# The first three blocks of a fused attention and MLP kernel, issued from one list of single operations

## The chip, the core and the metric

The kernel runs on one core of one Trainium2 chip. The core has four engines that matter here, each working through its own instructions in a fixed order: TensorE (PE in the profile) multiplies, VectorE (DVE) and ScalarE (ACT) do elementwise work, and SyncE (SP) issues the DMAs. They wait for one another through semaphores. The metric is the device time of one execution in microseconds. Before the change three runs took 893.93, 894.45 and 894.88 us, median 894.45.

## The reference

The input has 4 sequences of 576 positions, 8 heads of 64; together 2304 tokens of width 512. A windowed attention (each position sees itself and the 63 before it) is followed by two MLPs with a hidden width of 2048:

```python
mask = (rel >= 0) & (rel < 64)
attn = softmax(where(mask, q @ k.T / 8, -1e9));  x = attn @ v        # 2304 x 512
x = (maximum(x @ moe_w_in, 0) ** 2) @ moe_w_out
h = x @ moe2_w_in
out = where(h > 0, h, exp(minimum(h, 0)) - 1) @ moe2_w_out
```

The four weight matrices arrive as 64-bit floats, and the kernel decodes each one on the chip. Every matmul operand of the MLPs is split into a high and a low part, so one product is three matmuls (high by high, high by low, low by high).

## The kernel before

**Blocks.** The tokens go through in five blocks of 512, 256, 512, 512 and 512. The attention of a block is done in four head pairs ("groups" in the order list, numbered 0 to 19 over all five blocks). A group has its scores on PE (64 by 128 matmuls, `s_half`), a maximum of each 128 by 128 tile on DVE (`s_max`), the exponential on ACT (`s_exp`), the division on DVE, transposes on PE (`s_T`) with copies out of PSUM, the product with v on PE (`s_V`), and a split into high and low (`s_X`).

**First MLP.** The first three blocks go through the first MLP in the plain way, 16 chunks j of the hidden width each: `h_chunk` (4 of them, 12 matmuls) makes the hidden values in a PSUM bank, `h_relu`, `h_square` and the high half of `h_split` follow on ACT and the low half on DVE, and two chunks later `o_chunk` (4, 12 matmuls) adds the product with w_out onto four accumulators. From the sixth chunk of the first block on, every hidden chunk uses the same PSUM bank, so the hidden matmuls of the next chunk start only when the relu of this one has read the bank. The attention of blocks 4 and 5 is also done beside the third block, and those two blocks then go through the first MLP together, as seven products on sums of quarters instead of eight (`stepw`, operands `X`, results copied by ACT to tiles named `tl`). All later work, the rest of the first MLP and the second MLP, follows that.

**Weights of the second MLP.** Beside the blocks the kernel prepares weights in "portions" (`portions`, 105 of them): for each of 8 column pairs it forms seven quarter sums of the first MLP's w_in, and for each of 16 tasks it fetches a second-MLP weight in four pieces of 256 KB from DRAM into a landing place (a "lane"), decodes each (`high16` on ACT, `join` on DVE), forms sums on DVE, splits them (high on ACT, low on DVE) in a staging place and writes them back to DRAM. A piece's lane is fetched again as soon as it is decoded.

**What sets the order.** `FIRST` (line 950) is a written list of single operations for the first block's attention and its first six chunks. From there the loop at line 1078 emits code chunk by chunk: the four `h_chunk`, relu, square and split, a whole attention group (`group`, `turned`) at the chunks named in `GRP`, and whole portions (`slot`) as `SLOTS` says: 4 portions in the first block, 21 in the second and 30 in the third, of which 21 are in its last seven chunks:

```python
    SLOTS = {(0, NJ - 2): 2, (0, NJ - 1): 2}
    SLOTS |= {(1, j): 2 if j in (5, 6, 9, 10, 13) else 1 for j in range(NJ)}
    SLOTS |= {(TW, j): 1 if j < 9 else 3 for j in range(NJ)}
```

While `pinned` holds, every instruction is chained behind the one emitted before it on its engine (`Noted`), so each engine runs exactly in the order of emission; DMAs are chained on SP in the same way. A portion is emitted whole: its sums, its high parts and its low parts stand next to each other on DVE and ACT. Behind the third block the pins are off, and the framework's scheduler places the remaining portions among the `stepw` products. The lanes are half of the tile `top`, and two halves of `hw` from the third block on. At a block's end `leave1` copies the four accumulators to tiles (`e_tile`) and stores them to DRAM; two of the tiles share the two buffers named `g` with the relu's output.

Of the kernel before, what the change touches and what calls it, by code (L numbers as in the profile page):

```python
# [10 lines left out]
F32 = mybir.dt.float32  # L11
# [8 lines left out]
P = 128  # L20
# [3 lines left out]
ORDER2 = [0, 2, 3, 4, 1]  # L24

@with_exitstack
def window_attention_then_two_mlps(
# [224 lines left out]
    nf = [0]  # L252

    def fetch(x):
        if nf[0] < len(HALVES):
# [3 lines left out]
            lanes.append(x)  # L259

    def more_lanes(*ks):
        if lanes:
            for k in ks:
                fetch(hw[k // 2].bitcast(U16)[:, k % 2].rearrange("p (f w) -> p f w", w=4))

    def sub2(x, a, b, op=ALU.subtract):
        flush()
        vec.tensor_tensor(out=x, in0=a, in1=b, op=op)

    def put(i, p, k, x):  # L270

        m = x.shape[1]
        hi, lo, o = stage(m)
# [5 lines left out]
        def leave():  # L279
# [6 lines left out]
        if i == 1:  # L286
            for n in range(m):
                split(
                    *(z[:, n].rearrange("p (m a j) -> p a m j", m=FT, j=TB) for z in (hi, lo)),
                    x[:, n].rearrange("p (a m j) -> p a m j", m=FT, j=TB), vec,  # L290
                    leave if n == m - 1 else None,
                )
        else:
            split(hi, lo, x, vec, leave)

    def portions():

        y = lane["y"] = wts.tile([P, 2, KD * P], U32, tag="y", name="y")
# [3 lines left out]

        def sums(p, i):
            sub2(q21, q21, q22, ALU.add)
            sub2(q11, q21, q11)
            put(i, p, "s2", left)
            yield
            sub2(right, right, yf[:, 0:1, :HW].broadcast_to([P, 2, HW]))
            put(i, p, "s4", right)
            yield  # L310

        for p in range(NP):
# [3 lines left out]
            for k, j, h in (("a11", p, 0), ("a12", p, 1), ("a22", p + NP, 1)):  # L316
                sp.dma_start(
                    out=wd0[p][:, ORD1.index(k)], in_=wt[j, 0].bitcast(F32)[:, :, h * HW:(h + 1) * HW]
                )
            yield  # L320
            yield from sums(p, 2)
        fetch(top[:, 1].bitcast(U16).rearrange("p (f w) -> p f w", w=4))
        yield
        for n, (i, p) in enumerate(TASKS):
            for r in range(2):
                for h in range(2):
                    c = slice(h * HW, (h + 1) * HW)
                    x = lanes.pop(0)
                    high16(top[:, 0, c], x)

                    def rest(r=r, c=c, x=x):
                        join(y[:, r, c], top[:, 0, c], x)
                        fetch(x)

                    later(rest)
                yield
                flush()
            if i:
                put(i, p, 1, left)
                put(i, p, 3, yf[:, 1:2, HW:])  # L340
                yield
                sub2(q12, q12, q11)
                sub2(q22, q22, q12)
                put(i, p, 5, right)
                yield
                sub2(q11, q22, q11)
                sub2(q21, q21, q22)
                put(i, p, 7, left)
                yield
            else:  # L350
                put(i, p, "a11", yf[:, 0].rearrange("p (k f) -> p k f", k=2))
                put(i, p, "a22", yf[:, 1:2, HW:])
                yield
                yield from sums(p, i)
# [4 lines left out]
    def slot(n=1):  # L359
        for _ in range(n):  # L360
            if pinned:
                flush()
                if next(todo, 0) is None:
                    count[0] += 1
                continue
            with tc.issue_after(last["cd"].ins), tc.issue_after(last["ca"].ins):
                quiet.append(1)
                if next(todo, 0) is None:
                    count[0] += 1
                quiet.pop()  # L370
# [123 lines left out]
    def s_X(u):  # L494
        t, p = u
        n, ps = BLOCKS[t], st.pop(u)["v"]
        if t > TW:
# [3 lines left out]
            if p % 2:  # L501
                later(lambda: copy(XQ[k][:, 1], ps[:, :n], vec))
            else:
                copy(XQ[k][:, 0], ps[:, :n], act)
            return
        s = xs[t, p] = xp.tile([P, 2, NMAX], F32R, tag=f"xs{p}", name="xs")
# [74 lines left out]
    SLOTS = {(0, NJ - 2): 2, (0, NJ - 1): 2}  # L581
    SLOTS |= {(1, j): 2 if j in (5, 6, 9, 10, 13) else 1 for j in range(NJ)}
    SLOTS |= {(TW, j): 1 if j < 9 else 3 for j in range(NJ)}
    GRP = [(0, 4), (0, 6), (0, 8), (0, 10), (0, 12), (0, 13), (0, 15), (1, 3), (1, 7), (1, 11)]
    GRP = {x: n for n, x in enumerate(GRP + [(TW, j) for j in range(8)])}

# [17 lines left out]

    turn = [0, 0]

    def stage(m):

        n = turn[1] = turn[1] + 1
        if lw or hw:  # L610
            if n % 3 == 0 and hw:
                o = hw[1].rearrange("p y f -> p (y f)").rearrange("p (k y f) -> p k y f", k=2, y=2)
            elif lw:
                o = lw[0].tile([P, 2, 2, HW], F32R, tag="wo", name="wo", bufs=2)
            else:
                o = at.tile([P, 2, 2, HW], F32R, tag="wo", name="wo", bufs=1)
            o = o[:, :m]
            return o[:, :, 0], o[:, :, 1], o
        if n % 3 == 0:
            o = at.tile([P, 2, 2, HW], F32R, tag="wo", name="wo", bufs=1)[:, :m]  # L620
            return o[:, :, 0], o[:, :, 1], o
        k = 2 * (n % 3) - 2
        return *(xs[1, (k + r) % KD][:, :m, HW:] for r in range(2)), None
# [55 lines left out]
    def x_make(b, n=NH):  # L679
# [26 lines left out]
        yield  # L706

# [207 lines left out]
    def prod2(b, k, p, lo=0, hi=NH, ms=range(FT)):  # L915
# [28 lines left out]

    vec.memset(top, 0)
# [3 lines left out]
    U = [(0, p) for p in range(HP)]  # L949
    FIRST = """  # L950
        S00 S01 R000 R001 E000 R002 R010 E001 R011 S10 R003 E010 R012 S11 E011 R013 R100 E012 R101 R102
        E013 R110 R111 E110 R112 R103 E111 rc01 E002 D01 E003 top0 R113 T01 rc00 D00 pt01 stt0 E112 T00
        E113 S21 wh00 pt00 wl00 E100 V0 rc11 E101 D11 E102 E103 R210 T11 xhi0 rc10 D10 E210 pt11 R211
        T10 xlo0 E211 S31 pt10 R212 S20 R213 R310 E212 R311 V1 R312 E213 R313 R200 E310 rc21 E200 h00
        R201 D21 xhi1 E201 R202 T21 R203 E202 xlo1 E203 pt21 rc20 h01 D20 E311 S30 E312 T20 R300 E313
        R301 E300 R302 R303 E301 rc31 pt20 D31 E302 V2 E303 top1 rc30 T31 D30 xhi2 stt1 T30 pt31 xlo2
        pt30 wh10 top2 h02 wl10 V3 stt2 h10 xhi3 h11 xlo3 top3 h12 wh21 wl21 h03 wh20 h13 rl0 wl20 h20
        sq0 stt3 gh0 h21 rl1 h22 gl0 top4 h23 wh30 wl30 o00 sq1 wh31 o01 wl31 gh1 o02 rl2 stt4 o03 sq2
        h30 wh41 gh2 h31 gl1 top5 h32 gl2 h33 wl41 o10 wh40 rl3 wl40 o11 sq3 stt5 gh3 o20 o12 wh51 top6
        o13 wl51 o21 wh50 gl3 o22 wl50 o23 stt6 o30 o31 wh60 o32 wh61 wl61 o33 wl60 h40 h50 h51 h52 h53  # L960
        h41 h42 h43 rl4 sq4 gh4 rl5 gl4 sq5 gh5 gl5
    """.split()
    LOADS = {
        "": "0k 0q 1k 1q c 0v w0 2q 2k w1 1v 3q 3k w2 2v w3 3v w4 w5 w6",
        "V1": "4q 4k w7 4v w8 5q 5k w9 5v w10 w11 w12 w13 w14",
        "stt3": "w15 w16",
    }

    def loads(x):
        for x in LOADS.get(x, "").split():  # L970
            if x == "c":
                constants()
            elif x[0] == "w":
                w_load(int(x[1:]))
            else:
                u_load(order[int(x[0])], x[1])

    pinned.append(1)
    loads("")

    def first(x):
        k, a = x.rstrip("0123456789"), [int(i) for i in x.lstrip("abcdefghijklmnopqrstuvwxyzERSTDVX")]
        if k in ("S", "R", "E", "rc", "D", "T", "pt", "V", "xhi", "xlo"):
            u, bank_ = U[a[0]], lambda n=0: ps_o.tile([P, 512], F32, tag=f"o{2 * (a[0] % 2) + n}", name="pa")
        if k == "S":
            s_half(u, a[1], bank_(a[1]))
        elif k in ("R", "E"):
            (s_max if k == "R" else s_exp)(u, *a[1:])
        elif k in ("rc", "D"):
            (s_rc if k == "rc" else s_div)(u, a[1])  # L990
        elif k == "T":
            s_T(u, a[1], bank_(a[1]))
        elif k == "pt":
            s_pt(u, a[1], act)
        elif k == "V":
            s_V(u, bank_())
# [311 lines left out]
```

## Time and profile before

| | us |
|---|---|
| median of three runs | 894.45 |
| the profiled execution | 894.42 |
| its span, first to last instruction | 892.6 |
| PE busy | 832.6 |
| DVE busy | 600.4 |
| ACT busy | 560.9 |

The mean granted clock of PE is 0.971 of full. The profile cuts the span into stretches: the stretch from 0 to 52.25 us is the written list up to the output chunks of the first block's fourth chunk, 149.40 is the first block's end, 228.00 the second's, 356.06 the third's, and at 370.51 the third product of the last two blocks starts. A stretch's busy time on PE can't be read as work done: matmuls overlap in the records, and their recorded length grows when PE waits inside a group. The distance from the start of one group of matmuls to the start of the next, where nothing waits, is the time that the group really takes.

### The profile page before, as it was taken

The page shows a single profiled execution, that of the slowest core. Times are in us where ns is not written, and L with a number is a line of the kernel's source. Part 1 is how long each engine was busy: PE and PEld are TensorE (multiplying, and loading weights), DVE is VectorE, ACT ScalarE, POOL GpSimd, SP SyncE. Part 2 cuts the span into 40 slices and gives each one's busy share as a digit, 9 for nine tenths or more (in the row PEclk, how much of TensorE's full clock was granted, in tenths as well). Part 3 has the DMA queues.
Part 4 walks back from the last instruction along what each step waited for, and adds up shares of the span by engine and source line. Part 5 has one row for each costly group of instructions (what it writes and reads, how often), then busy time and mean ns, then how long its engine had stood idle before and what let it go on. Part 6 is the DMA issues. An engine that isn't in the chain of part 4 may idle for free. (4 is left out here: it accounts for less than half of the span.)

```text
span 892.6 us, 14761 instructions
## 1 busy us (share of the span) xinstructions
PE 832.6 (93%) x5196; PEld 748.0 (84%) x5196; DVE 600.4 (67%) x1403; ACT 560.9 (63%) x1279; POOL 2.1 (0%) x11
## 2 busy tenths in 40 slices
PE   6969997979999966499999999999999999999998
PEld 6757787979888745388888789999999999999998
DVE  6857876666555355657567674769956698666875
ACT  6845665655776354487777555776747766477652
POOL 0000000000000000000000000000000000000000
PEclk9989999998999978699999999999999999999999
DMA  9960127576653564599897969788898778777842
GB/s 346 401 246 28 59 80 249 190 260 216 207 179 96 194 230 156 187 355 357 309 343 253 337 234 311 276 312 265 271 299 272 285 267 277 247 249 289 287 155 54
DMA packets 98682, 214.86 MB, mean 241 GB/s; under 512 B 26544, under 2 KB 53680, under 8 KB 90160
## 3 DMA queue, kind: packets, MB, share of 16 engines
q1 hardware_dynamic: 97776, 213.72, 68.8%
q8 instruction: 41, 0.67, 0.3%
q10 hardware_dynamic: 832, 0.20, 0.1%
q14 instruction: 33, 0.27, 0.1%
HBM read 160.41 MB, written 53.48 MB: 240 GB/s over the span
## 5 line engine op out<-in xcount | busy, mean ns | idle before, releaser
L58 PE MATMUL o<-gs,w 128*128 128x512 f32 (+1 forms) x960 | 223.1, 378 | 1.8 <-ACT ev L58 1.2
L58 PEld LDWEIGHTS o<-gs,w 128*128 128x128 f32 x960 | 168.0, 190 | 35.9 <-ACT ev L58 1.6
L58 PE MATMUL po<-g,wr 128*128 128x384 f32 (+1 forms) x972 | 168.6, 333 | 0.0
L58 PEld LDWEIGHTS po<-g,wr 128*128 128x128 f32 x972 | 167.4, 188 | 0.0
L58 PE MATMUL ph<-xs,w 128*128 128x512 f32 (+1 forms) x576 | 129.7, 376 | 33.2 <-ACT g L58 25.9
L58 PEld LDWEIGHTS ph<-xs,w 128*128 128x128 f32 x576 | 101.1, 199 | 54.4 <-ACT g L58 27.8
L58 ACT ACTIVATE g<-gr 128x384 fp32r<-128x384 f32 x168 | 87.1, 525 | 55.4 <-PE po L58 49.4
L58 DVE TENSOR_TENSOR g<-gr,g 128x384 fp32r<-128x384 f32 x168 | 89.9, 551 | 16.1 <-ACT g L58 15.2
L58 PE MATMUL px<-xo,wr 128*128 128x384 f32 x432 | 83.8, 334 | 0.0
L58 PEld LDWEIGHTS px<-xo,wr 128*128 128x128 f32 x432 | 75.8, 188 | 0.4
L58 DVE TENSOR_TENSOR gs<-g,gs 128x512 fp32r<-128x512 f32 (+1 forms) x64 | 39.8, 623 | 47.5 <-ACT gs L58 47.0
L58 ACT ACTIVATE g<-ph 128x512 f32<-128x512 f32 (+1 forms) x48 | 24.9, 519 | 65.0 <-PE ph L58 54.6
L58 ACT ACTIVATE pb<-pb,nm 128x128 f32<-128x128 f32 x144 | 55.9, 390 | 10.4 <-DVE nm L58 9.4
L58 ACT ACTIVATE sy<-px 128x384 f32<-128x384 f32 x69 | 33.8, 490 | 43.5 <-PE px L58 43.1
L58 PE MATMUL px<-xo,w 128*128 128x512 f32 x192 | 48.2, 399 | 12.9 <-ACT tl L58 12.9
L58 PE MATMUL po<-xo,wr 128*128 128x384 f32 x288 | 56.2, 334 | 0.0
L58 PE MATMUL py<-xo,wr 128*128 128x384 f32 x288 | 55.7, 334 | 0.0
L58 PEld LDWEIGHTS px<-xo,w 128*128 128x128 f32 x192 | 37.1, 194 | 21.3 <-ACT tl L58 13.3
L58 DVE CUSTOM_DVE_ANT_0 pb<-pa,mask 128x128 f32<-128x128 f32 x144 | 32.7, 287 | 29.7 <-PE pa L58 29.6
L58 DVE TENSOR_TENSOR gr<-gr 128x384 f32<-128x384 f32 x96 | 52.1, 552 | 0.5
L58 DVE TENSOR_TENSOR gr<-sy,py 128x384 f32<-128x384 f32 x48 | 26.6, 554 | 36.8 <-PE py L58 23.5
L58 PEld LDWEIGHTS po<-xo,wr 128*128 128x128 f32 x288 | 50.5, 188 | 0.0
(88 smaller groups left out, 1116.9 us busy)
## 6 DMA issues: line engine op xcount, KB each, us to landing
wr<-wd SPq DMA_DIRECT2D x66, 1024.0 KB, 6.3
wd<-wo SPq DMA_DIRECT2D x38, 512.0 KB, 4.3
wr<-wd SPq DMA_DIRECT2D x24, 768.0 KB, 4.6
w<-wd SPq DMA_DIRECT2D x56, 256.0 KB, 5.3
vr<-in_v_dram SPq DMA_DIRECT2D x16, 512.0 KB, 5.2
wraw<-in_moe_w_in_dram SPq DMA_DIRECT2D x16, 511.8 KB, 8.7
wraw<-in_moe_w_out_dram SPq DMA_DIRECT2D x16, 511.8 KB, 9.9
wd<-tl SPq DMA_DIRECT2D x15, 512.0 KB, 4.5
```

The source lines that it names most:

```text
L58: r = fn(*a, **kw)
```

## The change

The written list now covers everything to the end of the third block. `ORDER1` names about 1,500 single operations with their numbers: `Lq.6` loads q of group 6, `S`, `R`, `E`, `rc`, `D`, `T`, `pt`, `V` (or `G`, scores of one group and the v product of another) and `xhi`, `xlo` are an attention group's steps, `top`, `stt`, `wh`, `wl` decode and split a weight unit of the first MLP, `H`, `rl`, `sq`, `gh`, `gl`, `O` are the steps of a chunk (numbered 0 to 47 over three blocks), `ev` and `st` copy and store an accumulator, `P.n` is the n-th single operation of the portions, and `X.n` of the operands of `stepw`. Each is emitted in the list's order and pinned behind its predecessor on its engine. `portions` now gives up control after every operation instead of after every portion.

```diff
+ORDER1 = """
+Lq.0 Lk.0 Lk.1 Lq.1 Lq.3 Lq.2 Lv.3 Lv.1 Lk.3 Lk.2 Lw.0 S.0.1 Lv.0 Lw.1 S.0.0 R.0.1.0 Lw.2 R.0.1.1
...
-    def more_lanes(*ks):
-        if lanes:
-            for k in ks:
-                fetch(hw[k // 2].bitcast(U16)[:, k % 2].rearrange("p (f w) -> p f w", w=4))
+    def lanes_of(kind, x):
+        for k in range(2):
+            fetch((kind, x[:, k * 2 * HW:(k + 1) * 2 * HW].bitcast(U16).rearrange("p (f w) -> p f w", w=4)))
...
+                    high16(top[:, 0, c], x[1])
+                    yield 0
+                    join(y[:, r, c], top[:, 0, c], x[1])
+                    fetch(x)
+                    yield h
...
+    def act_ev(t, m):
+        wait["e", t, m] = e_tile(t, m)
+        copy(wait["e", t, m][:, :BLOCKS[t]], acc[0][m][:, :BLOCKS[t]], vec if m % 2 else act)
...
+    def act_in(k):
+        x = wts.tile([P, 2, 2 * NMAX], F32R, tag=f"in{k}", name="tl")
+        lanes_of(f"in{k}", x[:, 1])
+        lend[f"in{k}"] = x[:, 0].rearrange("p (k y f) -> p k y f", k=2, y=2)
+        places.insert(0, f"in{k}")
+
+    def act_ret():
+        for k in (1, 2):
+            retired.append(f"in{k}")
+            places.remove(f"in{k}")
...
+        "pt": lambda g, n: s_pt(order[g], n, vec if g >= PTD and n else act),
...
+        "H": lambda q, c: h_chunk(*its[q], c, q if q < 4 else int(q == 5)),
...
+    for x in ORDER1.split():
+        name, *a = x.split(".")
+        ACTS[name](*map(int, a))
     assert not wait and not soon
...
-    unit(7)
-    for i, (t, j) in enumerate(its):
...
+    leave1(TW)
     pinned.clear()
     behind2[:] = [last["pe"]]
+    tl.update({k: lw[0].tile([P, NMAX], F32, tag=f"tl{k}", name="tl") for k in (1, 6, 7)})
+    for i in (1, 2):
+        stepw(0, i)
+        slot()
```

Besides the order, the list opens two further weight tiles of the third block (`in1`, `in2`) once their weights are used up, each as two lanes and one staging place (seven lanes in all until `ret`, three after it), and the half rows of the second block's `xs` tiles serve as two staging places from the first portion on. From group 8 on the second copy out of the transposes goes to DVE. 62 portions lie in the list instead of 55. The first two `stepw` products, which stood inside the third block's last chunk, come behind the list. One PSUM bank for the hidden chunks stays as it was.

On ACT near the third block's end, before: `xo<-xr` is an operand of `stepw`, `top<-` decodes a piece, `wo<-y` and `tl<-y` are high parts of a portion, and `g<-ph` is the relu.

```order
L58 ACTIVATE xo<-xr 128x1024 x2
L58 ACTIVATE wo<-y 128x2x256
L58 ACTIVATE wo<-y 128x256
L58 ACTIVATE g<-ph 128x512
L58 ACTIVATE g<-g 128x512
L58 ACTIVATE gs<-g 128x512
L58 ACTIVATE tl<-y 128x2x256
L58 ACTIVATE wo<-y 128x2x256
L58 ACTIVATE top<-top 128x256
L58 ACTIVATE top<-tl 128x256
L58 ACTIVATE g<-ph 128x512
L58 ACTIVATE g<-g 128x512
```

In the list's order, the same engine some chunks earlier in the third block, where the portions' work now lies:

```order
L167 ACTIVATE g<-ph 128x512
L167 ACTIVATE wo<-y 128x256
L167 ACTIVATE g<-g 128x512
L167 ACTIVATE gs<-g 128x512
L167 ACTIVATE xo<-xr 128x1024
L167 ACTIVATE pb,sm<-pb,nm 128x128 x4
L167 ACTIVATE pt<-pa 128x512
L167 ACTIVATE pb,sm<-pb,nm 128x128 x4
L167 ACTIVATE tl<-y 128x2x256
L167 ACTIVATE g<-ph 128x512
L167 ACTIVATE g<-g 128x512
L167 ACTIVATE gs<-g 128x512
```

Two operands of `stepw` and two high parts stood in a row ahead of the first relu here, and four more operations ahead of the next. Now one operand and one high part stand between a split and the next relu, with an attention group's tiles (`pb`, `pt`) between them, and one high part between a relu and its square. Counted over the third block's sixteen relus, the operations of portions and `stepw` between a relu and the one before it were 0 to 2 up to the twelfth chunk and then 8, 4, 7 and 5; now they are 0, 1 and from the third chunk on 2 to 5.

ACT behind the last chunk's split, before, up to the store copies (`ev<-o`) of the accumulators; `tl<-px` is the copy of a `stepw` product:

```order
L58 ACTIVATE top<-tl 128x256 x2
L58 ACTIVATE xo<-xr 128x1024 x3
L58 ACTIVATE tl<-px 128x512
L58 ACTIVATE wo<-y 128x2x256
L58 ACTIVATE wo<-y 128x256
L58 ACTIVATE tl<-y 128x2x256
L58 ACTIVATE tl<-px 128x512
L58 ACTIVATE top<-top 128x256
L58 ACTIVATE top<-tl 128x256
L58 ACTIVATE wo<-y 128x2x256
L58 ACTIVATE ev<-o_2535 128x512
L58 ACTIVATE ev<-o_2537 128x512
```

The same place now:

```order
L167 ACTIVATE wo<-y 128x2x256
L167 ACTIVATE top<-tl 128x256 x3
L167 ACTIVATE tl<-px 128x512
L167 ACTIVATE xo<-xr 128x1024
L167 ACTIVATE top<-top 128x256
L167 ACTIVATE g<-g 128x512
L167 ACTIVATE tl<-px 128x512
L167 ACTIVATE g<-g 128x512
L167 ACTIVATE gs<-g 128x512
L167 ACTIVATE xo<-xr 128x1024
L167 ACTIVATE wo<-y 128x2x256
L167 ACTIVATE tl<-y 128x256
```

The copies `ev<-o` of the accumulators now follow eleven rows below the last one shown. Between the first copy of a product and them stand 21 operations, the copies of three more products among them; before it were seven, with one more product.

## Rows read from the trace of the kernel before

**Rows 1.** Waits of PE over the whole span: who waited for whom, total, times, longest.
```profile
PE ph L58 <- ACT g L58: 25.9, 7, 8.0
PE px L58 <- ACT tl L58: 12.9, 1, 12.9
```
**Rows 2.** Busy time of each engine by stretch; x counts instructions; PEclk is the granted clock.
```profile
0.00:52.25 52.25, 43.56 (x383) 35.19 (x384) 41.67 (x137) 35.65 (x97) 2.10 (x11) 1.00 0.99 379
52.25:149.40 97.15, 89.69 (x617) 71.84 (x615) 69.39 (x190) 60.82 (x149) 0.00 (x0) 0.96 0.32 105
149.40:228.00 78.60, 68.37 (x600) 64.06 (x600) 47.92 (x135) 43.17 (x121) 0.00 (x0) 0.91 0.64 220
228.00:356.06 128.06, 112.36 (x858) 90.67 (x857) 66.69 (x210) 75.05 (x200) 0.00 (x0) 0.93 0.51 174
356.06:370.51 14.45, 1.54 (x7) 0.94 (x5) 7.35 (x10) 5.91 (x10) 0.00 (x0) 0.73 0.49 163
...
370.51:530.10 159.59, 158.39 (x673) 128.34 (x674) 105.53 (x219) 113.18 (x237) 0.00 (x0) 0.98 0.90 318
530.10:892.60 362.50, 358.71 (x2065) 356.93 (x2063) 261.84 (x505) 227.10 (x467) 0.00 (x0) 1.00 0.75 254
```
**Rows 3.** Timeline of PE in the second block: start, busy, operation, count, [idle before].
```profile
159.07 1.58 PE L58 MATMUL ph<-xs,w 128*128 128x256 f32 x12
160.50 1.58 PE L58 MATMUL o<-gs,w 128*128 128x256 f32 x12
...
163.78 1.59 PE L58 MATMUL pa<-kr,qd 64*64 64x128 f32 x32
165.30 1.15 PE L58 MATMUL pa<-pt,vr 128*64 128x64 f32 x32
166.38 0.98 PE L58 MATMUL o<-gs,w 128*128 128x256 f32 x6
167.21 1.03 PE L58 MATMUL pa<-ident,pb 128*128 128x128 f32 x8
168.00 0.61 PE L58 MATMUL o<-gs,w 128*128 128x256 f32 x3
...
171.93 1.69 PE L58 MATMUL ph<-xs,w 128*128 128x256 f32 x12 [0.48 <-ACT g L58]
```
**Rows 4.** Timeline of PE at the third block's end and behind it.
```profile
303.25 2.96 PE L58 MATMUL o<-gs,w 128*128 128x512 f32 x12
306.05 2.96 PE L58 MATMUL ph<-xs,w 128*128 128x512 f32 x12
...
381.57 2.88 PE L58 MATMUL px<-xo,w 128*128 128x512 f32 x12
```
**Rows 5.** Timeline of ACT after the first block's end.
```profile
154.19 0.38 ACT L58 ACTIVATE g<-ph 128x256 f32<-128x256 f32 x1 [5.92 <-DMA x2d<-ev]
```
**Rows 6.** Timeline of all engines at the third block's end.
```profile
316.09 0.49 ACT L58 ACTIVATE top<-tl 128x256 f16<-128x256 bf16 x1 [8.73 <-DMA tl<-in_moe_w_in_dram]
...
319.16 0.58 ACT L58 ACTIVATE g<-ph 128x512 f32<-128x512 f32 x1
...
319.79 5.49 PE L58 MATMUL ph<-xs,w 128*128 128x512 f32 x12 [7.97 <-ACT g L58]
...
341.46 5.00 PE L58 MATMUL ph<-xs,w 128*128 128x512 f32 x12 [7.73 <-ACT g L58]
...
369.88 0.58 ACT L58 ACTIVATE tl<-px 128x512 f32<-128x512 f32 x1
...
370.51 2.93 PE L58 MATMUL px<-xo,w 128*128 128x512 f32 x6 [12.91 <-ACT tl L58]
```
**Rows 7.** Groups of DVE instructions that prepare one weight unit: shape, count, busy, mean ns.
```profile
L58 DVE TENSOR_TENSOR w<-y,w 128x512 fp32r<-128x512 f32 x32 | 22.1, 692 | 1.0
...
L58 DVE SCALAR_TENSOR_TENSOR y<-wraw,top 128x1024 uint32<-128x1024 uint32 (+1 forms) x17 | 19.8, 1162 | 6.4 <-ACT top L58 6.0
...
L58 DVE CAST w<-y 128x512 fp32r<-128x512 f32 x32 | 13.5, 423 | 0.5
```

More of the change, by code (lines that the diff above doesn't have):

```diff
@@ L252, in window_attention_then_two_mlps, with fetch @@
     nf = [0]
-    def fetch(x):
-        if nf[0] < len(HALVES):
+    retired = []
+    def fetch(lane):
+        kind, x = lane
+        if nf[0] < len(HALVES) and kind not in retired:
             i, p, r, h = HALVES[nf[0]]
@@ L277, in put, with part, source, high @@
         )
-        def leave():
+        at_ = []
+        def part(z, n):
+            if i == 1:
+                return z[:, n].rearrange("p (m a j) -> p a m j", m=FT, j=TB)
+            return z
+        def source(n):
+            return x[:, n].rearrange("p (a m j) -> p a m j", m=FT, j=TB) if i == 1 else x
+        N = m if i == 1 else 1
+        def high(n):
+            if n == 0:
+                at_.append(stage(m))
+            act.activation(out=part(at_[0][0], n), in_=source(n), func=AF.Copy)
+        def low(n):
+            hi, lo, o = at_[0]
+            vec.tensor_tensor(
+                out=part(lo, n), in0=source(n), in1=part(hi, n).bitcast(F32), op=ALU.subtract
+            )
+            if n < N - 1:
+                return
             if o is None:
@@ L284, in leave @@
                 sp.dma_start(out=d, in_=o.bitcast(F32))
[L286 to L294, printed above, removed]
+        return [(high, n) for n in range(N)], [(low, n) for n in range(N)]
     def portions():
-        y = lane["y"] = wts.tile([P, 2, KD * P], U32, tag="y", name="y")
+        for p in range(KD):
+            if (1, p) not in xs:
+                xs[1, p] = xp.tile([P, 2, NMAX], F32R, tag=f"xs{p}", name="xs")
+        y = wts.tile([P, 2, KD * P], U32, tag="y", name="y")
         yf = y.bitcast(F32)
@@ L301, in portions, with run @@
         left, right = yf[:, :, :HW], yf[:, :, HW:]
+        def run(ops, end=0):
+            for k, (f, *a) in enumerate(ops):
+                f(*a)
+                yield end if k == len(ops) - 1 else 0
         def sums(p, i):
[L304 to L310, printed above, removed]
+            h, l = put(i, p, "s2", left)
+            yield from run([(sub2, q21, q21, q22, ALU.add), (sub2, q11, q21, q11)] + h)
+            wide = yf[:, 0:1, :HW].broadcast_to([P, 2, HW])
+            yield from run([(sub2, right, right, wide)] + l, 1)
+            h, l = put(i, p, "s4", right)
+            yield from run(h + l, 1)
         for p in range(NP):
@@ L359, in slot @@
     def slot(n=1):
[L360 to L363, printed above, removed]
-                    count[0] += 1
[L365 to L370, printed above, removed]
+        with tc.issue_after(last["cd"].ins), tc.issue_after(last["ca"].ins):
+            quiet.append(1)
+            while True:
+                x = next(todo, None)
+                if x is None:
+                    count[0] += 1
+                if x != 0:
+                    break
+            quiet.pop()
     CH = KD // 2
@@ L603, in e_tile @@
         return at.tile([P, 512], F32, tag="pt", name="ev", bufs=4)
[L605 to L623, printed above, removed]
     hw = []
@@ L1130, in window_attention_then_two_mlps, with s_bank, act_S, act_G @@
-    flush()
+    lwx = ctx.enter_context(ExitStack())
+    wait = {}
+    todo_x = x_first()
+    def s_bank(g, n):
+        return ps_o.tile([P, 512], F32, tag=f"o{2 * (g % 2) + n}" if g < HP else f"b{2 + n}", name="pa")
+    def act_S(g, *ns):
+        for a in ns or (0, 1):
+            s_half(order[g], a, s_bank(g, a))
+    def act_G(n):
+        if HP + n < len(order):
+            act_S(HP + n)
+        if n > 1:
+            s_V(order[HP + n - 2], spot(1, "pa"))
+    def act_xhi(g):
+        s_X(order[g])
+        if soon:
+            wait[g] = soon.pop()
@@ new lines, in act_gh, with act_st, act_hw @@
+    def act_gh(q):
+        h_split(*its[q])
+        wait["g", q] = soon.pop()
+    def act_ev(t, m):
+        wait["e", t, m] = e_tile(t, m)
+        copy(wait["e", t, m][:, :BLOCKS[t]], acc[0][m][:, :BLOCKS[t]], vec if m % 2 else act)
+    def act_st(t, m):
+        sp.dma_start(out=x2d[t][:, m, :], in_=wait.pop(("e", t, m))[:, :BLOCKS[t]])
+    def act_hw():
+        hw.extend(wts.tile([P, 2, NMAX], F32R, tag=f"w{k}", name="tl") for k in range(2))
+        lanes_of("hw", hw[0].rearrange("p y f -> p (y f)"))
+        lend["hw"] = hw[1].rearrange("p y f -> p (y f)").rearrange("p (k y f) -> p k y f", k=2, y=2)
+        places[:] = ["hw", "wo"]
```

421 lines of the change are left out of this document (212 added, 209 removed).

## The prediction

> **What bounds the kernel now.** I began with the waits of PE, because PE is the busiest engine. Two of them hold most of its idle time: the hidden matmuls wait 25.9 us in 7 places for ACT's relu (`g`), and one `stepw` product waits 12.9 us for ACT's copy `tl` [rows 1]. Then I read the stretches. From 530.10 to the end PE is busy 358.71 of 362.50 us, and from 370.51 to 530.10 158.39 of 159.59 [rows 2], so whatever the change can win lies ahead of about 381 us; the work behind that is the same in kind and amount, except that 43 instead of 50 portions are left for it.
>
> How much is lost ahead of it can't be read from busy time, so I counted PE's work by the distance between starts in places where nothing waits. Twelve matmuls of 512 columns take 306.05 - 303.25 = 2.80 us [rows 4]; twelve of 256 take 160.50 - 159.07 = 1.43; a full group's scores 165.30 - 163.78 = 1.52, its v products 1.08, its transposes 168.00 - 167.21 = 0.79 [rows 3]. The three blocks then need 64 sets of 2.80 (179.2), 32 of 1.43 (45.8), 16 full groups at 3.39 (54.2) and 4 half ones at 1.70 (6.8): 286.0 us, and 288.8 with the two `stepw` products that lie ahead of 370.51. PE got there at 370.5, so 81.7 us are lost. By stretch, with the work that the code's order puts in each:
>
> - 0 to 52.25: 4 groups and 8 sets, 36.0 us of work, 16.3 lost.
> - 52.25 to 149.40: 24 sets of 512 and 3.25 of 256, seven groups' scores, five v products and six groups' transposes, 85.9; lost 11.2.
> - 149.40 to 228.00: 28.75 sets of 256, 3.25 of 512, three groups, 60.4; lost 18.2.
> - 228.00 to 356.06: 28.75 sets of 512, half a set of `stepw`, six scores, eight v, seven transposes, 105.2; lost 22.9.
> - 356.06 to 370.51: half a set; lost 13.1. Behind it 36 matmuls take 381.57 - 370.51 = 11.06 instead of 8.40 [rows 4], since the stretch before had a mean granted clock of 0.73 [rows 2], partly at 1.2 GHz after the idle time: 2.7 more.
>
> The Trainium skill (Perfetto Trace Analysis, Identifying the Most-Contended Engine) says that matmul busy time is a poor measure because matmuls overlap in the trace. By busy time the five stretches hold 55.0 us of idle, 8.7 of them in the first; with the leftovers chosen below the sum would be 894.4 - 46.3 + 18.6 = 867. The start distances bear the page out, and I go by them.
>
> The causes are read at single places. At 316.09 ACT had waited 8.73 us for a fetched weight piece; the relu behind it ran at 319.16, and PE's hidden matmuls at 319.79 had waited 7.97. At 341.46 they waited again; at 370.51 PE had waited 12.91 for the copy that ACT ran at 369.88 [rows 6]. At 154.19 ACT's relu had waited 5.92 for the store of an accumulator tile, whose buffer it shares [rows 5]. In all of them ACT's queue is held by something that PE doesn't need.
>
> **The change part by part.** Nothing is computed more or less. What moves:
>
> The first stretch. The same operations up to the fourth chunk's output, and one more weight unit and hidden chunk ahead of it. DVE was busy 41.67 of 52.25 there [rows 2] and sets the pace; a unit costs it 1.16 + 2 x 0.42 + 2 x 0.69 = 3.4 us [rows 7], PE's extra chunk is 2.8 of useful work. Cost 0.6 (between -3, if the order starts earlier, and +3.4). Loads are issued in another order, but at the 379 GB/s of this stretch the 13 MB up to the weight unit that the fifth chunk needs are there by 35 us.
>
> The rest of the first block, 11.2 lost, mostly where the written list ended and whole weight units followed in ACT's and DVE's queues. Single operations take that away, but 33 operations of the portions come in where 11 were: 17 more on DVE. At 0.69 each that is 11.7 us; 69.39 + 11.7 - 3.4 for the unit moved ahead is 77.7 of the 85.9 that PE needs. At 90% of DVE some waits will show on PE: left over 0 to 11.2, I take 5, since in the first stretch PE lost something wherever DVE was that full.
>
> The second block, 18.2 lost. The store's wait goes: between that store and the relu that needs the buffer the list now has two chunks' outputs and a group's scores and v products (2 x 1.43 + 1.52 + 1.08 = 5.5 us of PE). The high parts that held the relu now lie singly behind it. Left over 0 to 10.6 (0.48 for each of 14 chunks as at 171.93 [rows 3], and the 3.9 that PE waited after the store): I take 3. One rule speaks against the change here: the Trainium skill (Perfetto Trace Analysis, Matmuls) wants independent matmul groups to rotate through PSUM banks, and the hidden chunks keep one bank. By it each chunk would expose the relu, 14 x 0.48 = 6.7, and the sum would be 849. The trace shows both, 0.48 idle at 171.93 and a full pace at 159.07; so only part is taken.
>
> The third block, 22.9 lost, nearly all behind 308: 21 of the 30 portions stood in its last seven chunks. They are now spread from the third chunk on, and a piece is fetched seven lanes ahead instead of three. A chunk's output set on PE covers 2.8 us of lateness, attention beside it up to 3.4 more. Left over 0 (as in the first ten chunks) to 22.9; I take 5, nearer the first because the same stretch ran without idle time while the portions were thin.
>
> The turn to `stepw`, 13.1 + 2.7 lost. Of the three wide operands (`xo`) right ahead of the first copy `tl` one is left, but the accumulators' copies `ev` stand 21 ACT operations behind that copy instead of 7, and the first output products of the next part need them. Twenty-one at 0.49 to 0.58 [rows 6] are 10 to 12 us, PE's nine products in between 9 x 1.4 = 12.6; a piece that lands late is added. Left over 0 to 15.8; I take 5.
>
> The 7 portions fewer behind it free some ACT and DVE time where PE lost 1.2 us: nothing. The second copy after the transposes on DVE adds 12 x 0.6 us to an engine with 67 of 128 us busy: nothing.
>
> Sum: 894.4 (the profiled execution's own time; the median is 894.45) - 68.1 (11.2 + 18.2 + 22.9 + 13.1 + 2.7) + 0.6 + 5 + 3 + 5 + 5 = 845. With all at their low ends it is 827, with all at their high ends 887.
>
> **The rivals.**
>
> *The late pieces stay.* The lanes are only three again behind `ret`, and SP issues in the list's order, so a fetch may stand behind a store that waits for DVE. For it speaks the 8.73; against it that the share of the DMA engines is 0.51 in this stretch [rows 2]. Then the third block and the turn keep their 38.7 and the rest 8.6: 894.4 - 68.1 + 47.3 = 874.
>
> *The list is too stiff: slower.* Between 228 and 370 some 32 decodes wait on ACT for a piece, each ahead of a relu, and the exponentials of the attention behind it feed DVE and PE too. If each came later than its cover, the loss is 32 times that: from 1.6 us on average the gain of 49 is gone, at 2.5 it is 845 + 80 = 925. For it: one order for four engines has no slack but what was put in; before, only the last seven chunks were exposed. Against: in 228 to 308 portions ran without any cost.
>
> *It doesn't do what it says.* DVE, not ACT's order, might set the pace of the first two blocks, with little gained: 894 if the third block loses as well what the others win.
>
> **How the numbers follow.** The forecast case (835 to 862) has 0.67, a time below 835 0.05, late pieces 0.17, no change to be told (within 0.2%, about 1.8 us, what a measurement of this kernel can tell) 0.03, slower 0.08. The range from 832 to 874 takes in the first rival's case as priced and leaves out less than 2 in 10. Faster: 0.67 + 0.05 + 0.17 = 0.89.
>
> **What would show it.** In the profile after: the third block's last output set at about 300 + 14 us instead of 356; PE's wait for ACT's `g` at under 8 us instead of 25.9; the wait for `tl` gone, and in its place a wait of output matmuls for `ev` of up to 5 us; a granted clock of 1.00 in nearly every stretch of 50 us; the stretch from there to the end as long as before, 520 us. The forecast is wrong if ACT still waits for fetched pieces by several us each, or if DVE is busy over 95% of the first 140 us and PE waits for it.

## The result and the profile after

The changed kernel took 841.09 us in the median of four runs (840.23 to 841.94), the kernel before 894.66 (four runs, 893.93 to 895.08). The ratio is 0.9402, with a 95% interval from 0.9386 to 0.9418: 53.6 us or 6.0% less. The profiled execution took 840.23 us; its span is 838.4, its mean granted clock 0.995 where it was 0.971. The forecast was 845.

The first view is again the waits of PE (who waited for whom, total, times, longest). These five are all there are:

```profile
PE py L167 <- DVE gb L167: 7.6, 2, 7.2
PE pa L167 <- DVE kr L167: 4.6, 1, 4.6
PE pa L167 <- DVE pb L167: 0.9, 2, 0.5
PE ph L167 <- ACT g L167: 0.7, 1, 0.7
PE ph L167 <- DVE w L167: 0.6, 1, 0.6
```

The 25.9 us that hidden matmuls waited for `g` and the 12.9 for `tl` [rows 1] have come down to 0.7 and to nothing. One new wait stands at the top: a `stepw` product waits 7.2 us for `gb`, which DVE makes. A third wait of before, which the rows ahead of the prediction don't show, has gone too (the 0.6 us for `w` above are at 27.84, in the first stretch):

```profile
PE ph L58 <- DVE w L58: 6.9, 1, 6.9
```

It stood at 65.11, where PE waited for the first weight unit behind the written list; with the hidden matmuls behind it, which took 4.77 us instead of 2.80, it is most of the 11.2 us that the rest of the first block lost.

The second view is the stretches of the changed kernel: from:to, length, busy time (x instructions) of PE, PEld, DVE, ACT and POOL, granted clock, DMA share, GB/s. The cuts are the same events as in [rows 2] as far as they exist: the fourth chunk's last output set ends at 55.06, the first block at 138.60, the third at 307.25 (200.00 is a mere cut); 330.62 is the first output product of the next part.

```profile
0.00:55.06 55.06, 48.99 (x396) 39.89 (x396) 45.45 (x143) 39.50 (x102) 2.12 (x11) 1.00 0.99 378
55.06:138.60 83.54, 82.85 (x589) 66.62 (x589) 71.72 (x197) 57.57 (x139) 0.00 (x0) 1.00 0.45 152
138.60:200.00 61.40, 61.40 (x611) 58.76 (x610) 42.64 (x128) 41.27 (x126) 0.00 (x0) 1.00 0.69 239
200.00:307.25 107.25, 107.25 (x857) 87.26 (x856) 78.09 (x233) 74.75 (x202) 0.00 (x0) 1.00 0.68 231
307.25:330.62 23.37, 16.12 (x61) 12.85 (x60) 15.20 (x28) 14.88 (x30) 0.00 (x0) 0.85 0.84 280
330.62:476.00 145.38, 145.07 (x629) 117.70 (x628) 90.03 (x188) 98.87 (x206) 0.00 (x0) 1.00 0.84 299
476.00:838.40 362.40, 358.24 (x2062) 356.45 (x2060) 260.61 (x503) 226.77 (x467) 0.00 (x0) 1.00 0.75 254
```

From 138.60 to 307.25 PE is busy all the time at full clock. The prediction warned against reading busy time as work, so I count by its paces: up to the end of the third block the list holds 286.0 us of work, of which 38.8 lie up to 55.06 (four groups, nine sets), 81.2 up to 138.60 and 166.0 behind that. The losses are then 55.06 - 38.8 = 16.3, 83.5 - 81.2 = 2.3, and 168.65 - 166.0 = 2.6, the last without a moment of idle time, so it may be the accuracy of the count or a pace slightly below the one taken. Five stretches lost 84.4 us before (16.3 + 11.2 + 18.2 + 22.9 + 15.8); now it is 31.0, with the turn. Behind it nothing has changed: from the first output product of the next part to the end it is 507.8 us, where it was 508.3 (from 384.29). The turn:

```profile
307.25 1.53 PE L167 MATMUL px<-xo,w 128*128 128x512 f32 x6
...
315.41 1.52 PE L167 MATMUL py<-xo,w 128*128 128x512 f32 x6
324.18 2.93 PE L167 MATMUL py<-xo,w 128*128 128x512 f32 x6 [7.25 <-DVE gb L167]
326.90 3.88 PE L167 MATMUL px<-xo,w 128*128 128x512 f32 x12
330.62 2.96 PE L167 MATMUL o<-gs,w 128*128 128x512 f32 x12
```

This is PE's timeline (start, busy, operation, count, idle before). Sixty matmuls of 512 columns between 307.25 and 330.62 are 13.6 us at 2.72 for twelve; they took 23.4. So 9.7 are lost, 7.25 of them waiting and 2.4 because six matmuls behind the wait take 2.72 instead of 1.36 and twelve 3.72 instead of 2.72. The granted clock of 324.18 to 326.90:

```profile
324.18:326.90 2.72, 2.72 (x6) 2.17 (x7) 0.00 (x0) 0.00 (x0) 0.00 (x0) 0.50 0.90 272
```

A clock of 0.50 is the lower of the two levels, 1.2 GHz, after 7.25 us without work; it stood at 1.00 ahead of the wait. A like price, 2.7 us, was paid before at 370.51, after 12.91 us.

Why DVE was late with `gb` is read from the timeline of ACT and DVE ahead of it:

```profile
317.64 1.15 DVE L167 TENSOR_TENSOR y<-y 128x256 f32<-128x256 f32 x2
...
318.94 0.69 DVE L167 TENSOR_TENSOR wo<-y,wo 128x512 fp32r<-128x512 f32 x1 [0.15 <-ACT wo L167]
...
320.56 0.63 ACT L167 ACTIVATE wo<-y 128x512 fp32r<-128x512 f32 x1 [1.14 <-DMA wd<-wo]
...
321.23 0.69 DVE L167 TENSOR_TENSOR wo<-y,wo 128x512 fp32r<-128x512 f32 x1 [1.59 <-ACT wo L167]
...
321.83 0.76 DVE L167 SCALAR_TENSOR_TENSOR y<-tl,top 128x256 uint32<-128x256 uint32 x2
...
323.44 0.68 DVE L167 TENSOR_TENSOR gb<-tl,py 128x512 f32<-128x512 f32 x1
```

Both inputs of `gb` were there by 317: `py` was done at 316.9 and the copies `tl` ran from 315.02 to 316.2. The addition ran at 323.44, since DVE had a portion's sums, two low parts (`wo`) and three decodes ahead of it in its queue, and one low part waited 1.59 us for ACT's high part, which itself waited 1.14 for the store of the staging place (`wd<-wo`). It is the mechanism of [rows 6] again, by three links instead of one, with DVE as the engine whose queue is held.

A second wait lies hidden behind this one. The copies `ev` of the accumulators, which the output products need, ran late too, behind a decode that had waited for a fetched piece:

```profile
327.07 0.49 ACT L167 ACTIVATE top<-tl 128x256 f16<-128x256 bf16 x1 [4.29 <-DMA tl<-in_moe_w_in_dram]
...
327.94 1.06 ACT L167 ACTIVATE ev<-o 128x512 f32<-128x512 f32 x2
```

Two more copies ran on DVE until 329.2. Without the wait for `gb` PE would have reached its first output product at about 320.9 (330.62 - 9.7, an estimate) and would have waited some 8 us for `ev` instead; no run shows this wait by itself.

### The profile page after: what moved, and what is told of

It is laid out like the page before. It is cut to its first block, busy times and chain, and to the rows that moved or that the text cites. A ratio compares the mean times of both kernels' runs of the same rounds, so it can differ in the third digit from the quotient of the medians.

```text
span 838.4 us, 14725 instructions
## 1 busy us (share of the span) xinstructions
PE 819.9 (98%) x5196; PEld 739.5 (88%) x5196; DVE 603.7 (72%) x1415; ACT 553.6 (66%) x1267; POOL 2.1 (0%) x11
## 4 chain that ended last, share of the span: by engine, by line
PE 94%; DMA 2%; DVE 1%; ACT 1%; issue 1%; POOL 0%; SPq 0%; POOLq 0%; ACTq 0%
PE po L167 26%; PE o L167 24%; PE px L167 14%; PE ph L167 13%; PE py L167 9%; PE pa L167 8%; DMA tl<-in_moe_w_out_dram 1%; DVE pb L167 1%; DMA tl<-in_moe_w_in_dram 1%; DMA wd<-wo 1%; DMA w<-wd 0%; ACT top L167 0%; ACT gb L167 0%; ACT pb L167 0%; ACT wo L167 0%
## 5 line engine op out<-in xcount | busy, mean ns | idle before, releaser
L167 PE MATMUL o<-gs,w 128*128 128x512 f32 (+1 forms) x960 | 218.1, 375 | 0.0
L167 PEld LDWEIGHTS o<-gs,w 128*128 128x128 f32 x960 | 166.3, 188 | 33.1 <-issue 0.2
L167 ACT ACTIVATE g<-gr 128x384 fp32r<-128x384 f32 x168 | 87.2, 526 | 55.3 <-PE po L167 48.9
L167 PE MATMUL ph<-xs,w 128*128 128x512 f32 (+1 forms) x576 | 121.9, 359 | 1.3 <-ACT g L167 0.7
L167 PEld LDWEIGHTS ph<-xs,w 128*128 128x128 f32 x576 | 95.5, 188 | 19.4 <-ACT g L167 1.1
L167 PEld LDWEIGHTS py<-xo,wr 128*128 128x128 f32 x288 | 50.4, 188 | 0.0
L167 PE MATMUL py<-xo,w 128*128 128x512 f32 x144 | 38.4, 403 | 7.6 <-DVE gb L167 7.6
```

The lines of the kernel that those rows point to most:

```text
L167: r = fn(*a, **kw)
```

## The experiments

**Are the late pieces the cause?** The changed kernel without the two further weight tiles as lanes and staging places, so three lanes all along:

```diff
     def act_in(k):
-        x = wts.tile([P, 2, 2 * NMAX], F32R, tag=f"in{k}", name="tl")
-        lanes_of(f"in{k}", x[:, 1])
...
+        return
     def act_ret():
         for k in (1, 2):
-            retired.append(f"in{k}")
-            places.remove(f"in{k}")
+            pass
```

> The changed kernel with its list as it is, but without the two extra weight tiles as landing and staging places: three lanes instead of seven, two staging places instead of four, in the third block. Theory A (what PE lost was the order on ACT: the relu stood behind whole portions): the list's order alone carries nearly all, 841 to 847 us, PE's wait for the relu (g) stays under 5 us. Theory B (what PE lost was pieces that landed late, and the extra lanes cure it): ACT waits for pieces by 2 to 8 us at many of the 32 decodes, 855 to 885 us.

Measured: 841.40 us (840.37 to 843.33), ratio 0.9401 (0.9369 to 0.9432). PE's waits, and ACT's for one kind of piece:

```profile
PE py L167 <- DVE gb L167: 6.4, 1, 6.4
...
PE px L167 <- ACT tl L167: 1.1, 1, 1.1
...
PE ph L167 <- ACT g L167: 0.7, 1, 0.7
```

```profile
ACT top L167 <- DMA tl<-in_moe_w_in_dram: 7.9, 4, 3.5
```

ACT waits more for pieces (7.9 us in four places for this kind, against 4.3 in one in the changed kernel, and another 4.3 for one that lands in `top`), yet PE's wait for the relu stays 0.7. The further lanes are worth nothing that can be measured; in the new order a held decode doesn't reach PE ahead of the turn. So the gain comes from the order, as far as the runs show: the half rows of `xs` as staging places and the second copy on DVE were not taken out by themselves.

**How much is the place of the portions worth by itself?** The kernel before, with the third block's whole portions spread evenly:

```diff
-    SLOTS |= {(TW, j): 1 if j < 9 else 3 for j in range(NJ)}
+    SLOTS |= {(TW, j): 2 if j < 14 else 1 for j in range(NJ)}
```

> The kernel before with one line changed: the third block's 30 whole portions at two a chunk instead of one in the first nine chunks and three in the last seven. Nothing else of the change. Theory A (crowding ahead of the relu): of the 22.9 us that the third block lost some 10 remain, and of the 13.1 behind it most remain, since the operands of the next part still stand there: 880 to 886 us. Theory B (late pieces with three lanes): the fetches are as short ahead as before, and the loss stays or spreads: 890 to 900 us.

Measured: 883.80 us (882.04 to 884.43), ratio 0.9869 (0.9832 to 0.9906). PE's waits:

```profile
PE ph L58 <- ACT g L58: 20.5, 9, 5.7
...
PE pa L58 <- DVE nm L58: 4.9, 8, 1.5
...
PE px L58 <- ACT tl L58: 2.3, 1, 2.3
```

The turn's 12.9 us go to 2.3, which is the whole gain of 10.7. The relu's waits only move: nine instead of seven, 20.5 us instead of 25.9, and transposes begin to wait for DVE's maxima (`nm`), as whole portions now stand beside attention groups. Ahead of the first of these waits, at 234.35, DVE's maxima stood behind a decode that had waited 3.72 us for ACT, which had waited 3.65 for a fetched piece. The time lies in the range expected of crowding, but by luck: there the third block was to give most of the gain and the turn to keep its loss.

**Is it the single operations or their place?** The changed kernel with each of its portions up to `P.191` emitted whole at the place of its first operation:

```diff
+            if lo <= n < hi:
+                if n in begins:
+                    done = begins[begins.index(n) + 1] - 1
+                    out += [f"P.{i}" for i in range(n, done + 1)]
...
+    for x in whole(ORDER1.split(), 0, 192):
```

> The changed kernel, but each portion of the list (P.0 to P.191) emitted whole at the place of its first operation; attention, weight units, lanes and staging as changed. Theory A: the relus of the second and third block stand again behind a portion's chain of sums on DVE and high parts on ACT, 1 to 3 us at a time: PE waits for g come back to 10 to 25 us, 850 to 870 us. Theory B (lanes and spreading are what counts, single operations are not): 841 to 845 us.

Measured: 849.90 us (848.91 to 850.69), ratio 0.9492 (0.9463 to 0.9522). PE's waits:

```profile
PE py L167 <- DVE gb L167: 11.6, 1, 11.6
...
PE ph L167 <- ACT g L167: 3.1, 4, 1.0
```

Breaking the portions up is worth 8.8 us. About half of that (11.6 - 7.2 = 4.4) shows at the turn, 2.4 at the relus, where 10 to 25 us of waits were expected to come back and 3.1 did. Five sixths of the gain stay. How much of them is the place that the list gives each block of work, and how much the single weight units and attention steps, was not taken apart beyond the next run.

**And the single operations of the first MLP's own weights?** In the changed kernel the weight units from the eighth on are emitted whole, at the place of the unit's last operation:

```diff
+            elif at[u] == n:
+                out += [f"top.{u}", f"stt.{u}"] + [f"{w}.{u}.{i}" for i in range(2) for w in ("wh", "wl")]
```

> The changed kernel, but the weight units from the eighth on (top, stt, wh, wl) emitted whole at the place of each unit's last operation, as the kernel before did; the rest of the list as it is. Theory A, for the first block (what it lost behind 52.25 us was whole units in ACT's and DVE's queues): PE waits for g or w come back, 4 to 9 us, 845 to 850 us. Rival (single operations don't matter here, only that the units no longer start in a heap at 58 us): 840 to 843 us.

Measured: 855.82 us (853.48 to 856.72), ratio 0.9568 (0.9548 to 0.9588), 14.7 more than the changed kernel and more than was expected. PE's waits, the stretch in which the unit work lies, and the first product behind the list:

```profile
PE pa L167 <- DVE nm L167: 9.7, 3, 3.8
PE py L167 <- DVE gb L167: 7.6, 1, 7.6
...
PE ph L167 <- ACT g L167: 0.7, 1, 0.7
```

```profile
55.00:138.60 83.60, 73.18 (x464) 57.10 (x464) 64.09 (x166) 48.85 (x112) 0.00 (x0) 0.96 0.35 119
...
320.31 1.53 PE L167 MATMUL px<-xo,w 128*128 128x512 f32 x6
```

The relu didn't suffer. A unit is 3.4 us of DVE in one piece [rows 7], and three attention groups had their maxima behind one: transposes waited 2.19, 3.79 and 3.75 us for `nm`. In the same time PE did 464 matmuls instead of 589. The list ends at 320.31 instead of 307.25, 13.1 us later, so nearly the whole loss of the profiled execution (13.3) lies here: 9.7 of waits, and the rest behind them, mostly at the lower clock (0.96 in the mean; the twelve hidden matmuls behind the first wait take 84.32 - 80.27 = 4.05 us instead of 2.80). So in the first block the order of DVE decides, as in the turn.

**What holds the turn?** First the changed kernel without the five `slot()` calls among the first `stepw` products:

```diff
-    for i in (1, 2):
+    for i in (1, 2, 6, 5, 7):
         stepw(0, i)
-        slot()
...
```

> The changed kernel without the five portions between the first five products behind the list (they run later, there are more places than portions). In the changed kernel PE waits 7.25 us at 316.9 for the DVE addition gb, which stands behind sums, low parts and decodes of portions, and loses some 2.4 more at the lower granted clock. Theory A (the scheduler puts those portions ahead of gb): the wait is gone, 831 to 835 us. Theory C (gb waits for its copy tl or its buffer, or the rest of the list's own portions is what stands ahead): 839 to 842 us.

Measured: 841.38 us (840.17 to 842.20), ratio 0.9397 (0.9368 to 0.9426); `gb` is waited for 7.6 us as before. The portions given out there are not the ones ahead of it. Then also without the list's own last twenty portion operations (from `P.195` on), which are done later instead:

```diff
     for x in ORDER1.split():
+        if x[:2] == "P." and int(x[2:]) > 194:
+            continue
```

> The changed kernel without the five portions between the first five products behind the list, and with the list's portions ending at P.194 instead of P.214, so that 20 operations (five portions) run later among the other products. The addition gb then has no portion's work ahead on DVE. Theory D (the list's own last portions held gb for 7.25 us, and PE lost 2.4 more at the lower granted clock): ratio to before 0.929 to 0.933, 831 to 835 us. Rival (what is put off is missed later, where the DMA engines are 0.84 to 0.91 busy and the remaining places are few): 838 to 843 us.

Measured: 832.14 us (831.35 to 832.77), ratio 0.9307 (0.9293 to 0.9321). The span is 830.0 us with a granted clock of 0.999. PE at the turn:

```profile
315.50 1.52 PE L167 MATMUL py<-xo,w 128*128 128x512 f32 x6
317.49 1.65 PE L167 MATMUL py<-xo,w 128*128 128x512 f32 x6 [0.47 <-DVE gb L167]
...
321.70 2.96 PE L167 MATMUL o<-gs,w 128*128 128x512 f32 x12
```

The first output product starts at 321.70 instead of 330.62, 8.9 us earlier, and that is the gain in the time: 8.95 by the medians, 8.5 by the ratios. The twenty operations had stood ahead of `ev` as well: its copies on ACT run at 314.28 instead of 327.94. From the first output product to the end it is 508.3 us against 507.8, so they cost next to nothing where they are done instead. This version beats both kernels. The further lanes were left out of it too:

> The version with the turn freed (832.1 us), without the two further weight tiles as lanes and staging places (three lanes all along). Theory A: the lanes are worth nothing anywhere, since in the changed kernel with three lanes PE's waits stayed; 831 to 833.5. Theory B: their price was hidden behind the wait of 7.25 us at the turn, which gave late pieces time; with that wait gone the pieces behind 310 us come late and PE waits 2 to 7 us more: 834 to 839, with PE waits for tl, w or g in the first 340 us.

Measured: 832.06 us (831.59 to 832.37), ratio 0.9308 (0.9295 to 0.9321): with the turn's wait gone, the lanes are still worth nothing; a wait of 1.5 us for `tl` shows, the one for `gb` doesn't.

**Would moving only the relu do?** The kernel before, with each chunk's whole portions emitted behind the next chunk's relu instead of ahead of it:

```diff
+        slot(carry)
+        carry = slots
...
-            if c == 1 and slots > 1:
-                slot()
```

> The kernel before with its whole portions, three lanes and the same number per chunk, only each chunk's portions emitted right behind the next chunk's relu instead of ahead of it. Theory A (the relu stood behind the portion's high parts, and the single hidden bank makes PE wait for it): the second block's 18.2 lost us fall to 6 to 10, the third's 22.9 to 8 to 14, the turn stays: 868 to 880 us. Rival (the portions' own length and late pieces hold the queues wherever they stand, the next relu is late instead): 885 to 895 us.

Measured: 889.74 us (nine runs, 887.28 to 892.54), ratio 0.9945 (0.9927 to 0.9964): 4 us won where 14 or more were expected; it lies in the rival's range. PE's waits:

```profile
PE ph L58 <- ACT g L58: 13.3, 3, 7.4
PE px L58 <- ACT tl L58: 9.7, 1, 9.7
```

Half of the relu's waits go, and the third `stepw` product starts at 355.40 instead of 370.51. Two things take it back. The waits that remain in the blocks come from other things that hold the relu: at 157.49 the store of [rows 5], and at 328.24 `stepw` operands that stand ahead of it and wait for DVE (start, busy, operation, idle before):

```profile
326.65 1.06 ACT L58 ACTIVATE xo<-xr 128x1024 fp32r<-128x1024 f32 x1 [2.55 <-DVE xr L58]
...
328.24 4.76 PE L58 MATMUL ph<-xs,w 128*128 128x512 f32 x12 [7.44 <-ACT g L58]
```

And of the 15.1 us by which the product came earlier 11.4 are lost behind it: 3.5 over the next 36 matmuls (14.58 us instead of 11.06 [rows 4]), and most of the rest around 520 us, where PE waits 4.3 us for operands `xo` and the clock of the stretch from 520 to 570 is 0.90. Which portion comes late there I did not follow up.

**What paces the first stretch?** It lost 16.3 us before and after, and I had put that down to DVE. The timeline of the changed kernel shows another candidate: PE's small matmuls take nearly twice as long there as later, 16 scores 14.58 - 12.68 = 1.90 us and 23.83 - 22.80 = 1.03, while the granted clock reads 1.00 in both places:

```profile
12.68 1.97 PE L167 MATMUL pa<-kr,qd 64*64 64x128 f32 x16
...
22.80 1.09 PE L167 MATMUL pa<-kr,qd 64*64 64x128 f32 x16
```

The version with the turn freed was run with 14 matmuls on a zeroed tile while PE waits for the first loads:

```diff
+    zz = sc.tile([P, NMAX], F32, tag="g", name="zz")
+    vec.memset(zz[:, :P], 0.0)
+    zp = ps_o.tile([P, 512], F32, tag="b0", name="zp")
+    for _ in range(14):
+        pe.matmul(out=zp[:, :P], lhsT=zz[:, :P], rhs=zz[:, :P], start=True, stop=True)
```

> The version with the turn freed (832.1 us), and ahead of everything 14 matmuls of 128 by 128 on a zeroed tile, which PE can do while it waits for the first loads (it starts its first scores at 4.63 us). Nothing uses their result. The question is what costs the 16.3 us of the first stretch. Theory A, the prediction's: DVE sets the pace there. Then an earlier start of PE changes nothing: the fourth chunk's last output set ends at 55 us as before, 831.5 to 833. Theory B: PE itself runs the first 15 us at half its later pace (16 scores take 1.90 us at 12.68 and 1.03 at 22.80, though the granted clock reads 1.00 in both), and the faster pace comes some time after its first work. Then it comes up to 3.6 us earlier, the scores behind it take half, and 1 to 3.5 us go: the set ends at 52 to 54 us, 829 to 831. Theory C: the half pace goes with the full DMA engines or the order of the loads; then the groups up to 20 us keep their lengths and nothing is won.

Measured: 831.58 us (831.02 to 831.76), ratio 0.9302 (0.9289 to 0.9314). PE's timeline, and a stretch:

```profile
5.99 2.96 PE L167 MATMUL pa<-kr,qd 64*64 64x128 f32 x64
10.40 0.63 PE L167 MATMUL pa<-ident,pb 128*128 128x128 f32 x4 [1.45 <-ACT pb L167]
12.05 1.08 PE L167 MATMUL pa<-ident,pb 128*128 128x128 f32 x4 [1.02 <-DVE pb L167]
13.07 1.97 PE L167 MATMUL pa<-kr,qd 64*64 64x128 f32 x16
```

```profile
12.68:22.00 9.32, 9.32 (x107) 7.95 (x105) 7.04 (x32) 7.24 (x26) 0.00 (x0) 0.52 1.04 408
```

The 64 scores now run at the later pace, 2.96 us instead of 5.52, though they start at 5.99 instead of 4.63, since the added matmuls outlast the loads. PE then stands 1.45 and 1.02 us for the exponential and the division, and from 12.68 to 22.00 the recorded clock is 0.52, with the same length of 1.97 for 16 scores as in the changed kernel. So the slow groups of the changed kernel are most likely at the lower clock level too, which its record doesn't show. Nothing is won: the fourth chunk's last output set ends at 55.3. With the two gaps filled by such matmuls as well:

```diff
+    fill(10)
...
+        fill({"S.1.1": 7, "T.0.1": 5}.get(x, 0))
```

> As the run with 14 early matmuls, but 10 of them ahead of the first scores, 7 between the first four score sets and the first transposes, and 5 between the first and the second transposes, where PE stood for 1.45 and 1.02 us there, after which the granted clock was 0.52 from 12.68 to 22.00. Theory A: the first stretch goes by the chain over DVE and ACT, and the half pace costs nothing; the fourth chunk's last output set ends at 55 us as before, 831 to 832.5. Theory B: the half clock costs it; from 12.7 to 22 PE does 4.5 us of paced work in 9.3 us. With the clock kept at 1.00 up to 4.7 us of that go, less what DVE's waits take back (DVE was busy 9.4 of the 10.6 us behind it): the set ends at 51 to 53.5 us, 827 to 830.

Measured: 830.60 us (829.72 to 831.65), ratio 0.9293 (0.9272 to 0.9313). PE's timeline:

```profile
12.78 1.09 PE L167 MATMUL pa<-kr,qd 64*64 64x128 f32 x16
14.81 0.65 PE L167 MATMUL pa<-ident,pb 128*128 128x128 f32 x4 [0.94 <-DVE pb L167]
...
17.79 3.26 PE L167 MATMUL pa<-pt,vr 128*64 128x64 f32 x64
...
54.33 0.68 PE L167 MATMUL pa<-kr,qd 64*64 64x128 f32 x16
```

The 16 scores that took 1.97 us take 1.09, but PE then waits for the division, and the clock falls again: it is 0.72 from 16.42 to 17.79 and 0.59 from 17.79 to 20.98, where the 64 products with v take 3.19 us instead of 2.01 as later in the same run (29.72 to 31.73). The stretch ends at 54.33 instead of 55.23 in the version with the turn freed: 0.9 us, which the times, whose intervals overlap with the run without these matmuls, can't tell from nothing. So about 1 us of the 16.3 came back, and the run doesn't show all that the clock costs, since it was not kept up. How the rest divides between the clock and the chain of loads, maxima, exponentials and divisions of the first four groups stays open. All of it lies ahead of 32.55, for from there on the changed kernel runs at full pace (96 matmuls in 22.6 us, 22.4 by the count), and that is where DVE is fullest: 21.65 of 22.51 us.

## Why the prediction was right

It was right in the mechanism and within 4 us of the time. Point by point:

- *Where the gain lies.* "whatever the change can win lies ahead of about 381 us": the losses counted ahead of the first output product fell from 84.4 to 31.0, 53.4 of the 54.2 us by which the span is shorter. The start-distance count carried this; by busy time the sum had been 867, 26 us too slow, as the records show PE busier than its work (55.0 us idle, 84.4 lost).
- *The first stretch, +0.6.* Measured 0.0: 16.3 lost in both. That DVE sets the pace is not borne out: the loss lies ahead of 32.55, and behind it, with DVE busy 21.65 of 22.51 us, PE lost nothing. How much is the clock and how much the chain over DVE and ACT stays open.
- *The rest of the first block, 5 left; the second block, 3; the third, 5.* These terms were mis-sized: 2.3, and 2.6 for the two others together, instead of 13. PE's wait for `g` is 0.7 us where under 8 was named. DVE at 86% from 55.06 to 138.60 (71.72 of 83.54) did not make PE wait, though I had taken 5 us at 90%, "since in the first stretch PE lost something wherever DVE was that full". The trace of before says otherwise: from 41.00 to 52.25 DVE was busy 10.71 of 11.25 us and PE kept its pace. That PE would wait for it, in another order, is shown by the run with whole weight units. For the second block the prediction had set 6.7 us as what a single PSUM bank might expose. The Trainium skill (Perfetto Trace Analysis, Matmuls) would have independent matmul groups rotate through different banks; in this trace the one bank cost next to nothing, no wait for `g` behind 138.60 and 2.6 us at most by the count.
- *The turn, 5 left.* Mis-sized the other way: 9.7 are left. The wait for `tl` went, as said, but in its place no output matmul waited for `ev`; the last products ahead of the output waited for `gb`. The copies `ev` were late all the same, by more than was counted: the 21 operations, put at 10 to 12 us, took from 309.4 to 327.9, and the wait for `gb` covered that. I had counted what stands ahead of `ev` on ACT and not what stands ahead of `gb` on DVE. The clock's 2.4 us behind the wait were not in the term at all, though the same price stood in the sum of before.
- *The rivals.* Late pieces do occur (4.3 us once, and 12.2 in five places with three lanes). They reached PE in the old order [rows 6]. In the new one they don't hold the relu, and at the turn the wait for `gb` covers the piece that held `ev`. "Too stiff" holds at the one place where the list ends with twenty operations that nothing near needs.
- *What would show it.* The third block ended at 307.25 instead of about 314, with 1.00 in every long stretch, and the part behind the turn is as long as before.

The ends of the sum, 827 and 887, leave out the first stretch's own range; with it they are 823 and 890. The misses cancel in part, so that the sum comes as close as 4 us is partly luck: the blocks came 8.1 us better, the turn 4.7 worse, the first stretch 0.6 better. The sum with the measured leftovers is 894.4 - 84.4 + 31.0 = 841.0, against 840.2 for the profiled execution.

## What to carry to other kernels

Count a stretch's loss by the distance between starts of like groups, not by idle time, and look for the instruction that holds an in-order queue: PE waited for operations that were ready but stood behind others. Breaking work into single operations pays where the long piece stands ahead of something that PE needs within its cover; at the end of such a list, look at what the last entries stand ahead of on each engine, not just on the one that was late before. In this kernel more buffers for late transfers were worth nothing that could be measured once the consumer of a transfer no longer stood ahead of the critical operation.

## What the runs showed of the hardware

- The granted clock reads 1.00 over the first 22 us of the changed kernel, while equal groups take 1.8 times as long as later (16 scores 1.90 and 1.03 us, 64 products with v 3.53 and 2.01). With matmuls ahead of them the record shows 0.52 for groups of the same length. A pace should be checked against the lengths of several like groups: 16 scores at 55.15 take 0.61 us at the same recorded 1.00, so not every such difference is the clock.
- From 12.68 to 55.06 us the changed kernel moved over 400 GB/s:

```profile
32.55:55.06 22.51, 22.51 (x100) 17.96 (x96) 21.65 (x33) 16.12 (x22) 0.00 (x0) 1.00 1.03 403
```

PE kept its full pace beside it.
